# A float32 product with the values for all sixteen units of the first chunk, and a later due step for the values' halves, in a clustered attention with an MLP

## The chip, the cores and the metric

The kernel runs on one core of a Trainium2 chip. The metric is the device time of one execution in microseconds (us), as a median of runs. The engines are named as the profile names them: PE is TensorE (matmul; PEld its weight loads), DVE is VectorE, ACT is ScalarE, POOL is GpSimd, and SP issues the DMAs.

## The reference

Attention with a mask: a query sees a key only if both fall to the same of 16 centroids. Its output, of all heads side by side, goes through a two-layer MLP whose nonlinearity is a scaled square of the relu.

```
q_assign = argmax(q_n @ c_n^T); k_assign = argmax(k_n @ c_n^T)    # q_n, k_n, c_n: normalised
mask = q_assign[:, :, :, None] == k_assign[:, :, None, :]
scores = where(mask, scale * (q @ k^T), -1e9)
attn = exp(scores - max(scores)); attn = attn / (sum(attn) + 1e-9)
x = (attn @ v) of all heads, reshaped to 3072 x 512
h = x @ w_in; r = max(h, 0); g = s * r * r + b; out = g @ w_out
```

Sizes: q, k and v have 4 batches, 8 heads, 768 positions and 64 elements a head; w_in is 512 x 2048 and w_out 2048 x 512. All is float32.

## The kernel before

**Units.** The attention is cut into 192 units of 128 queries of one head, in the order batch b, chunk c (256 positions, three a batch), head pair hp, tile t, head h. Sixteen units make a chunk of the MLP's input: 256 rows of x, 512 columns, of which each group of four units (one head pair) yields 128. The main loop runs over steps i. Step i takes the scores of unit i (L476: 4 matmuls of float16 halves, with the mask folded into them as a large number), their maxima (L486, DVE) and the exponentials p (L496, ACT).

**The MLP.** With a lag of 21 steps (`LAG`) a step of the MLP runs beside a unit: 192 steps, 16 for each chunk, one 128-column slice of the hidden layer each (`mlp_in` L632, `mlp_relu` L639 to L642, `mlp_gl` L647, `mlp_out` L659). The first step of a chunk needs x of all its four head pairs, and `mlp_start` (L617 to L623), which makes scales from the maxima of x.

**Float16 in halves.** What is multiplied is mostly split into a high and a low float16 half, with a power of two as scale, and three products of halves replace one in float32. The weights are fetched in 32 pieces (SP), rebased (L215, ACT), narrowed (L219 and L220, DVE) and bounded (L227 and L229, ACT, with L232 on PE for w_in). When all are bounded, their scale is set (L254 to L259 for w_in, L263 to L269 for w_out, small instructions on DVE), and from step 17 on each is split (`wsplit`: L277 on ACT, L279 on DVE, two pairs a step for 16 steps).

**The values.** `prep_v` loads v (tiles `vn`, four head pairs of two heads), takes the maximum, and splits each pair into `vh` (L194, ACT) and `vl` (L196, DVE). For the first batch the raw `vn` are also kept as `VN`.

**Probabilities times values.** Three forms of it exist:

- Units 0 to `RAW` - 1, that is 0 to 3 here: p is turned by six PE transposes in float32 into `turned` (L520, two halves of three), each half is copied into the float32 tile `PT` (first half by DVE, second by ACT, L126 and L128 in the helper `copy`), and six float32 matmuls a unit multiply it with `VN` (L542). The sum of p comes out of the exponentials as a second output of ACT, read by an extra instruction; `finish_x` scales the group's x by an extra ACT instruction (L592).
- Units `RAW` to `TURN` - 1, 4 to 15: p is turned in the same way, but each half is copied to a float16 high half by ACT (L525), and DVE subtracts that from `turned` for the low half (L526). Eighteen float16 matmuls a unit (L547 to L549) use `vh` and `vl`; a column of ones in `vh` gives the sum.
- Units from 16 on: p is split by ACT or POOL or DVE (L126, L128, L528) and turned by a DMA; `value` (L574 to L576) follows.

`values` takes two units at a time, four steps behind (L555, L556 and L559 on DVE normalise). `finish_x` then splits x (L596 ACT, L599 POOL), turns it by a DMA (L602) and takes its maximum (L105).

**What sets the order.** A scheduler that simulates the program's time writes each engine's queue; the engines run their queues in order, and tiles come out of pools with fixed numbers of buffers. The two lines that say when the halves of the values are due are of `prep_v`: for batch 0 the pairs go in the order 1, 2, 3, 0, one a step; for later batches a pair waits for its step, `yield from until(...)`, in which a generator gives its turn back until the loop's step counter is there.

Of the kernel before, what the change touches and what calls it, by code (L numbers as in the profile page):

```python
# [26 lines left out]
def tile_cluster_attention_mlp(ctx, tc, q, k, v, cent, w_in, w_out, s_in, b_in, out):  # L27
# [5 lines left out]
    NP = H // 2  # L33
# [9 lines left out]
    LAG = 21  # L43
    BIGN = 11

    RAW = 4
    TURN = 16
    URGENT = 20

# [10 lines left out]
    def floor2(eng, dst, src):  # L60
        eng.tensor_scalar(dst, src, 2.0 ** -60, 2.0 ** 60, op0=ALU.max, op1=ALU.min)
        eng.tensor_scalar(dst.bitcast(I32), dst.bitcast(I32), EXPMASK, None, op0=ALU.bitwise_and)

    def inverse2(eng, dst, src, e):
        eng.tensor_scalar(dst.bitcast(I32), src.bitcast(I32), -1, (254 + e) << 23, op0=ALU.mult, op1=ALU.add)
# [15 lines left out]
    def load(dst, src, free=False):  # L81
        if last_transpose[0] is None or free:
            nc.sync.dma_start(dst, src)
        else:
            with tc.issue_after(last_transpose[0].ins):
                nc.sync.dma_start(dst, src)
# [4 lines left out]
    def columns(n, name):  # L91
        return sb.tile([P, n], BF16, tag=f"amb{n}", name=f"amb_{name}", bufs=3)

    def allmax(dst, src, name, bank="m"):
        n = src.shape[1]
        if bank == "turned":
            pm = turned[:, 0]
        else:
            pm = (ps_m if bank == "m" else ps_h).tile([P, 512], F32, tag=bank, name=f"am_{name}")
        for j in range(n):  # L100
            nc.tensor.matmul(pm[:, j * P : (j + 1) * P], src[:, j : j + 1].broadcast_to([P, P]), identb, start=True, stop=True)
        V.tensor_reduce(dst, pm[:, : n * P].rearrange("p (n q) -> p n q", q=P), axis=AX.X, op=ALU.max)

    def absmax(dst, src, axis=AX.X):
        V.tensor_reduce(dst, src, axis=axis, op=ALU.max, apply_absolute_value=True)  # L105
# [18 lines left out]
    def copy(eng, dst, src):  # L124
        if eng is A:
            A.activation(dst, src, AF.Copy)  # L126
        else:
            eng.tensor_copy(dst, src)  # L128
# [58 lines left out]
    def split(hi, lo, src, f, early):  # L187
        if early:
            A.activation(src, src, AF.Copy, scale=f)
            last_split[1] = A.activation(hi, src, AF.Copy)  # L190
            yield
            G.tensor_tensor(lo, src, hi, op=ALU.subtract)
        else:
            last_split[1] = A.activation(hi, src, AF.Copy, scale=f)  # L194
            yield
            last_split[0] = V.scalar_tensor_tensor(lo, src, f, hi, op0=ALU.mult, op1=ALU.subtract)  # L196
# [112 lines left out]
    def until(k):  # L309
        while step[0] < k:  # L310
            yield
# [106 lines left out]
    def prep_v(b):  # L418
        vm = sb.tile([P, 8], F32, tag="vm", name=f"vm_{b}", bufs=2)
        VM[b] = vm  # L420
        vns = []
        for hp in range(NP):
            vn = sb.tile([P, 2, T, D], F32, tag="kv", name=f"vn_{b}_{hp}", bufs=5)
            load(vn, v[b, 2 * hp : 2 * hp + 2].rearrange("h (p t) d -> p h t d", t=T), False)
            vns.append(vn)
            if b == 0:
                VN[hp] = vn
            yield
        if b:
            yield from until(START[b][3])  # L430
        for hp in range(NP):
            absmax(vm[:, hp : hp + 1], vns[hp].rearrange("p h t d -> p (h t d)"))
            if hp < NP - 1:
                yield
        vc = columns(1, f"v{b}")
        V.tensor_reduce(vc, vm[:, 0:NP], axis=AX.X, op=ALU.max)
        if b:
            yield
        allmax(vm[:, 5:6], vc, f"v{b}")
        yield  # L440
        floor2(V, vm[:, 6:7], vm[:, 5:6])
        inverse2(V, vm[:, 7:8], vm[:, 6:7], 0)
        V.tensor_scalar(vm[:, 7:8], vm[:, 7:8], 2.0 ** 13, None, op0=ALU.mult)
        V.tensor_scalar(vm[:, 6:7], vm[:, 6:7], 2.0 ** -19, None, op0=ALU.mult)
        for hp in ((1, 2, 3, 0) if b == 0 else range(NP)):
            vh = sb.tile([P, 2, T, D + 2], F16, tag="vh", name=f"vh_{b}_{hp}", bufs=5)
            vl = sb.tile([P, 2, T, D], F16, tag="vl", name=f"vl_{b}_{hp}", bufs=5)
            VS[(b, hp)] = (vh, vl)
            G.memset(vh[:, :, :, D:], 1.0)
            yield from split(vh[:, :, :, :D], vl, vns[hp], vm[:, 7:8], False)  # L450
            if b == 0 or hp < NP - 1:
                yield
                if b > 0:
                    yield from until(48 * b - 8 + 4 * hp)
# [33 lines left out]
    def exps(i):  # L488
# [5 lines left out]
        p = sb.tile([P, S], F32, tag="big", name=f"p_{i}", bufs=BIGN)  # L494
        total = {"accum_out": sm[:, 2, j : j + 1]} if i < RAW else {}
        last_exp[0] = A.activation(p.rearrange("p (a b) -> p a b", a=2), u["sc"], AF.Exp, bias=bi, scale=u["scale"], **total)  # L496
# [11 lines left out]
    def low(i):  # L508
        u = U[i]
        if i < TURN:  # L510
            n = T // 2
            flat = sb.tile([P, T * P], F32, tag="big", name=f"PT_{i}", bufs=BIGN) if i < RAW else None
            two = None if i < RAW else sb.tile([P, 2, T * P], F16, tag="big", name=f"PT_{i}", bufs=BIGN)
            if i < RAW:
                u["PT"] = flat.rearrange("p (n q) -> p n q", n=T)
            else:
                u["PT"] = two.rearrange("p e (n q) -> p (e n) q", q=P)
            for e in range(2):
                for kt in range(n):
                    nc.tensor.transpose(turned[:, e, kt * P : (kt + 1) * P], u["p"][:, (e * n + kt) * P : (e * n + kt + 1) * P], ident)  # L520
                cols = slice(e * n * P, (e + 1) * n * P)
                if i < RAW:
                    copy((V, A)[e], flat[:, cols], turned[:, e, : n * P])
# [8 lines left out]
    def values(i):  # L532
# [3 lines left out]
        for e in range(2):  # L536
            b, c, hp, t, h = units[i + e]
            PT = U.pop(i + e)["PT"]
            o = px[:, e * W : e * W + D]
            if i < RAW:  # L540
                for kt in range(T):
# [144 lines left out]
    for b in range(B):  # L686
        for c in range(NCH):
            for hq in range(2):
                s0 = ((b * NCH + c) * 2 + hq) * 8 - 10
                if s0 > 0:  # L690
                    at(s0, prep_q(b, c, hq))
        if b > 0:
            at(START[b][0], prep_k(b, 0))
            at(START[b][1], prep_v(b))
            for hp in range(1, NP):
                at(48 * b - 24 + 6 * hp + (hp == NP - 1), prep_k(b, hp))
# [13 lines left out]
    def prepare(k):  # L710
# [4 lines left out]
        with behind(last_score[0], last_exp[0], last_max[0]):  # L715
# [9 lines left out]
            if k == 4:  # L725
                some(first_v, 1)
                active.append(first_v)

    first_v = prep_v(0)
    first_k = [prep_k(0, hp) for hp in range(NP)]  # L730
    first_q = [prep_q(0, 0, hq) for hq in range(2)]
# [91 lines left out]
```

## Time and profile before

| | |
|---|---|
| runs | 946.06, 946.23, 949.96 us; median 946.23 |
| profiled execution | 952.97 us, its span 951.3 us |
| busy in the span | PE 830.0 us (87%), ACT 715.4 (75%), DVE 651.1 (68%), POOL 548.0 (58%) |
| mean granted clock of PE | 0.954 of full speed |

A row of a group gives line, engine, operation, tiles written and read, shapes and count, then busy time and the mean length in ns, then the idle time of the engine just ahead of these instructions, with what ended most of it. A row of the timeline gives start and length in us; what stands in brackets is the idle time before it and what ended that. In the chain of work that ended last, each row is a piece of the path that led to the end. The page's forty slices of the span show how the start differs from the rest:

```profile
PE   0565667886999889999999989999999899999997
DVE  7689978798786766758967766667877565654100
PEclk9975697999999999999999999999999999999999
```

Each digit is a fortieth of the span (23.8 us) in tenths, of busy time, and in the last row of the clock that PE was granted.

### The profile page before, as it was taken

Reading aid. Unit: us, or ns where it says so; the run is one execution under the profiler, and the core shown is the slowest. Engines: PE = TensorE matmul, PEld = TensorE weight load, DVE = VectorE, ACT = ScalarE, POOL = GpSimd, SP = SyncE. Lnnn points to the kernel's source line nnn. Section 1 sums busy time; section 2 is a strip of 40 time slices with the busy share of each in tenths; the row PEclk is TensorE's granted clock in tenths of the full one; section 3 lists DMA queues with packets and bytes.
Section 4 is the critical chain, followed back from the end, with each engine's and each line's share of the span. In section 5 each row is a group of like instructions: output and inputs, shape, how many; then the busy total and the mean of one; then the engine's idle time right before and its main releaser. Section 6 shows DMA issues by size and latency. Waiting matters only on the chain.

```text
span 951.3 us, 22936 instructions
## 1 busy us (share of the span) xinstructions
PE 830.0 (87%) x8697; PEld 580.1 (61%) x8697; DVE 651.1 (68%) x1684; ACT 715.4 (75%) x1405; POOL 548.0 (58%) x580
## 2 busy tenths in 40 slices
PE   0565667886999889999999989999999899999997
PEld 0353445554676657767666657667766676676764
DVE  7689978798786766758967766667877565654100
ACT  3469866777688678788878868888888788888543
POOL 3010115667577567677677747767776676666321
PEclk9975697999999999999999999999999999999999
DMA  5898513767897897876887978979968777577200
GB/s 165 215 262 283 161 38 80 174 145 150 168 168 146 172 204 123 167 162 139 178 169 164 201 156 148 171 145 197 178 140 182 145 123 159 115 140 140 46 23 23
DMA packets 437759, 144.25 MB, mean 152 GB/s; under 512 B 405392, under 2 KB 434064, under 8 KB 437648
## 3 DMA queue, kind: packets, MB, share of 16 engines
q1 hardware_dynamic: 437648, 142.78, 70.7%
q8 instruction: 68, 1.11, 0.5%
q14 instruction: 43, 0.35, 0.1%
HBM read 35.69 MB, written 6.29 MB: 44 GB/s over the span
## 4 chain that ended last, share of the span: by engine, by line
PE 45%; DVE 23%; DMA 12%; ACT 7%; issue 5%; POOL 2%; SPq 1%; POOLq 0%; DVEq 0%; ACTq 0%
PE h L632 16%; PE acc L659 16%; PE sc L476 6%; DVE ssm L486 5%; DMA qn<-in_q_dram 3%; DMA PT<-ph 2%; PE sc L574 2%; DMA kn<-in_k_dram 2%; DMA vn<-in_v_dram 2%; PE sc L576 2%; PE sc L575 2%; ACT p L496 1%; DVE wis L279 1%; DVE qa L196 1%; DMA wst<-in_moe_w_in_dram 1%
## 5 line engine op out<-in xcount | busy, mean ns | idle before, releaser
L528 POOL TENSOR_TENSOR ph<-p,ph 128x768 f16<-128x768 f32 x176 | 297.0, 1688 | 129.7 <-ACT ph L126 71.1
L632 PE MATMUL h<-x,wis 128*128 128x256 f16 x2304 | 291.9, 276 | 16.1 <-ACT r L639 9.7
L659 PE MATMUL acc<-wos,gs 128*128 128x512 f16 x1152 | 299.7, 381 | 4.1 <-POOL gs L647 2.8
L632 PEld LDWEIGHTS <-wis 128*128 128x128 f16 x2304 | 222.5, 99 | 72.3 <-issue 18.0
L496 ACT ACTIVATE p<-sc,ssm,qsm 128x768 f32<-128x768 f32 x192 | 188.5, 982 | 2.0
L647 POOL TENSOR_TENSOR gs<-r,gs 128x256 f16<-128x256 f32 x192 | 136.5, 712 | 88.1 <-ACT r L642 79.4
L486 DVE TENSOR_REDUCE ssm<-sc 128x1 f32<-128x768 f32 x192 | 181.7, 947 | 2.8 <-PE sc L476 2.6
L659 PEld LDWEIGHTS <-gs 128*128 128x128 f16 x1152 | 101.4, 98 | 79.4 <-POOL gs L647 5.6
L493 ACT ACTIVATE ssm<-ssm,lift,qsm 128x1 f32<-128x1 f32 x192 | 73.1, 381 | 91.3 <-DVE ssm L486 90.1
L126 ACT ACTIVATE ph<-p 128x768 f16<-128x768 f32 x164 | 136.7, 833 | 1.3 <-DMA PT<-ph 0.2
L639 ACT ACTIVATE r<-h,cf 128x256 f32<-128x256 f32 x192 | 89.2, 465 | 57.8 <-PE h L632 54.5
L574 PE MATMUL sc<-vh,PT 128*128 128x65 f16 x1032 | 117.4, 195 | 6.9 <-DMA PT<-ph 6.8
L576 PE MATMUL sc<-vh,PT 128*128 128x65 f16 x1032 | 117.9, 193 | 0.0
L575 PE MATMUL sc<-vl,PT 128*128 128x64 f16 x1032 | 117.5, 192 | 0.0
L476 PE MATMUL sc<-KA,QA 128*128 128x384 f16 x384 | 98.9, 340 | 19.2 <-ACT p L496 13.8
L574 PEld LDWEIGHTS <-PT 128*128 128x128 f16 x1056 | 99.1, 98 | 22.8 <-DMA PT<-ph 10.1
L575 PEld LDWEIGHTS <-PT 128*128 128x128 f16 x1056 | 98.5, 99 | 11.8 <-issue 0.5
L476 PE MATMUL sc<-KB,QB 128*128 128x384 f16 x384 | 99.2, 340 | 6.9 <-DMA QB<-qb 6.9
L576 PEld LDWEIGHTS <-PT 128*128 128x128 f16 x1056 | 98.7, 97 | 1.3
L580 DVE TENSOR_SCALAR ssm<-sc 128x1 f32<-128x1 f32 x172 | 26.1, 152 | 84.5 <-PE sc L576 83.7
L642 ACT ACTIVATE r<-r 128x256 f32<-128x256 f32 x192 | 78.8, 410 | 2.9
L641 ACT ACTIVATE gs<-r 128x256 f16<-128x256 f32 x192 | 78.9, 411 | 2.7
(176 smaller groups left out, 1145.0 us busy)
## 6 DMA issues: line engine op xcount, KB each, us to landing
wst<-in_moe_w_in_dram SPq DMA_DIRECT2D x16, 512.0 KB, 5.1
kn<-in_k_dram SPq DMA_DIRECT2D x16, 384.0 KB, 4.3
qn<-in_q_dram SPq DMA_DIRECT2D x24, 256.0 KB, 3.3
vn<-in_v_dram SPq DMA_DIRECT2D x16, 384.0 KB, 4.3
out_dram<-o SPq DMA_DIRECT2D x12, 512.0 KB, 3.6
wst<-in_moe_w_out_dram SPq DMA_DIRECT2D x8, 512.0 KB, 5.7
gs<-in_moe_w_out_dram SPq DMA_DIRECT2D x8, 512.0 KB, 4.9
PT<-ph SPq DMA_TRANSPOSE x176, 3.4
```

What stands on the lines that cost most here:

```text
L126: A.activation(dst, src, AF.Copy)
L476: last_score[0] = nc.tensor.matmul(sc[:, e, :HALF], X[:, col, :], y[:, h * S + e * HALF : h * S + (e + 1) * HALF], start=st, stop=not st)
L486: last_max[0] = V.tensor_reduce(SM[i // 4][:, 0, j : j + 1], U[i]["sc"], axis=AX.XY, op=ALU.max, negate=True)
L496: last_exp[0] = A.activation(p.rearrange("p (a b) -> p a b", a=2), u["sc"], AF.Exp, bias=bi, scale=u["scale"], **total)
L528: G.tensor_tensor(u["ph"][:, 1, :], u["p"], u["ph"][:, 0, :], op=ALU.subtract)
L574: nc.tensor.matmul(o1, PT[:, kt, :], vh[:, h, kt, : D + 1], start=(kt == 0), stop=False)
L575: nc.tensor.matmul(o, PT[:, kt, :], vl[:, h, kt, :], start=False, stop=False)
L576: nc.tensor.matmul(o1, PT[:, T + kt, :], vh[:, h, kt, : D + 1], start=False, stop=(kt == T - 1))
L632: nc.tensor.matmul(ph[:, :CW], WSP[ft][0][:, wl, kt, :], XS[(b, c, kt)][:, :, xl, :], start=(i == 0), stop=(i == len(terms) - 1))
L639: A.activation(r, ph[:, :CW], AF.Relu, scale=MS[(b, c)][0])
L647: G.tensor_tensor(g[:, 1, :], r, g[:, 0, :], op=ALU.subtract)
L659: nc.tensor.matmul(acc[:, t, :], g[:, gl, rows], WSP[ft][1][:, wl, :], start=(ft == 0 and gl + wl == 0), stop=(ft == NF - 1 and gl == 1))
```

## The change

`RAW` becomes 16, the value of `TURN`. So all sixteen units of the first chunk take the first of the three forms: their halves of `turned` are copied once instead of copied and subtracted, `PT` is float32, six float32 matmuls a unit take the place of eighteen in float16, the sums come with the exponentials, and x of all four groups is scaled in `finish_x`. The second form has no unit left. For batch 0, `prep_v` takes the head pairs in the order 0 to 3, and the halves of pair hp are due from step `RAW - 2 + 2 * hp` on, that is 14, 16, 18 and 20; the last pair of batch 0 no longer yields behind its split. The first unit that uses the halves is unit 16, of pair 0.

```diff
-    RAW = 4
+    RAW = 16
...
-        for hp in ((1, 2, 3, 0) if b == 0 else range(NP)):
+        for hp in range(NP):
+            if b == 0:
+                yield from until(RAW - 2 + 2 * hp)
             vh = sb.tile([P, 2, T, D + 2], F16, tag="vh", name=f"vh_{b}_{hp}", bufs=5)
             vl = sb.tile([P, 2, T, D], F16, tag="vl", name=f"vl_{b}_{hp}", bufs=5)
...
-            if b == 0 or hp < NP - 1:
+            if hp < NP - 1:
                 yield
```

The lines below it in the file stand two lines lower afterwards (L526 becomes L528, and so on). Where the change moves instructions in the engines' queues is shown at the places that the prediction speaks of.

## The prediction

> **What bounds the kernel now.** I first cut the run into stretches and read each engine's busy time there (columns: start and end, length, then busy time and instruction count of each engine, the granted TensorE clock, DMA share and GB/s).
>
> ```profile
> core 0: us, PE busy (x) PEld busy (x) DVE busy (x) ACT busy (x) POOL busy (x), PEclk, DMA share, GB/s
> 60.00:117.60 57.60, 35.02 (x284) 27.04 (x284) 50.78 (x132) 47.45 (x98) 6.12 (x8) 0.59 0.75 222
> 117.60:151.20 33.60, 20.08 (x203) 13.95 (x203) 27.16 (x69) 20.63 (x39) 8.79 (x8) 0.80 0.19 43
> 151.20:232.00 80.80, 68.42 (x696) 45.83 (x695) 70.71 (x152) 60.57 (x119) 50.66 (x44) 0.95 0.65 140
> 232.00:951.30 719.30, 684.80 (x7304) 478.79 (x7304) 455.32 (x1209) 557.06 (x1096) 470.54 (x476) 0.99 0.74 147
> ```
>
> From 232 us on TensorE is busy for 684.80 of 719.30 us: that part has its own length and follows the MLP's start. Before it VectorE (DVE) is the fullest engine, and TensorE is idle for 36.1 of the 91.2 us from 60.00 to 151.20. The cuts are events of the timeline:
>
> ```profile
> 113.30 0.67 DVE L220 SCALAR_TENSOR_TENSOR wo<-gs,wo 128x512 uint32<-128x512 uint32 x1
> 116.82 0.14 DVE L259 TENSOR_SCALAR glob<-glob 128x1 f32<-128x1 f32 x1
> 147.53 1.20 SPq L602 DMA_TRANSPOSE x<-xn  x1
> 151.18 0.46 ACT L639 ACTIVATE r<-h,cf 128x256 f32<-128x256 f32 x1
> ```
>
> The last weight is narrowed at 113.30 and the scale of w_in stands at 116.82, yet the MLP's first relu runs at 151.18, behind the transpose of x at 147.53: x of units 12 to 15 comes last, not the weights. The chain of work that ended last shows why, in a piece from between:
>
> ```profile
> 120.67 0.48 ACT PT L525
> 121.17 0.57 DVE PT L526
> 121.79 0.56 PE turned L520 x3
> 122.37 0.50 ACT PT L525
> 122.89 0.56 DVE PT L526
> 123.45 0.86 DVE ssm L486
> 124.31 0.16 DVE ssm L555
> 124.50 0.17 DVE ssm L556
> 124.66 0.52 DVE PT L526
> 125.23 0.55 PE turned L520 x3
> ```
>
> Each half of a unit's probabilities goes TensorE, ScalarE (ACT), VectorE and back, with nothing beside it: 121.17 to 122.89 is 1.72 us a half, 3.4 a unit, and VectorE's queue lies in that loop.
>
> **The change, part by part.** Prices are from the groups by line and shape from 36 to 160 us (count, busy us, mean ns, idle time ahead):
>
> ```profile
> L486 DVE TENSOR_REDUCE ssm<-sc 128x1 f32<-128x768 f32 x21 | 19.9, 949 | 2.8 <-PE sc L476 2.6
> L526 DVE TENSOR_TENSOR PT<-turned,PT 128x384 f16<-128x384 f32 x24 | 13.2, 550 | 2.4 <-ACT PT L525 2.3
> L525 ACT ACTIVATE PT<-turned 128x384 f16<-128x384 f32 x24 | 11.6, 483 | 7.4 <-PE turned L520 6.5 <-DVE glob L62 0.8
> L128 DVE COPY PT<-turned 128x384 f32<-128x384 f32 x4 | 2.2, 547 | 1.8 <-PE turned L520 1.8
> L126 ACT ACTIVATE PT<-turned 128x384 f32<-128x384 f32 x4 | 1.9, 476 | 0.7 <-PE turned L520 0.7
> L496 ACT ACTIVATION_READ_ACCUMULATOR p<-sc,ssm,qsm 128x1 f32 x4 | 0.8, 192 | 0.0
> L592 ACT ACTIVATE xs<-xs,vm 128x256 f32<-128x256 f32 x1 | 0.5, 493 | 0.0
> ```
>
> Neighbours on an engine overlap a little, so I charge the distance of starts:
>
> ```profile
> 126.45 0.56 DVE L526 TENSOR_TENSOR PT<-turned,PT 128x384 f16<-128x384 f32 x1
> 126.93 0.95 DVE L486 TENSOR_REDUCE ssm<-sc 128x1 f32<-128x768 f32 x1
> 127.79 0.14 DVE L65 TENSOR_SCALAR glob<-glob 128x1 int32<-128x1 int32 x1
> ```
>
> that is 0.48 for a half's turn and 0.86 for a reduce, both about 0.1 under their lengths.
>
> *VectorE.* 24 subtractions leave, 12 plain copies come, at one price each: 12 x 0.48 = 5.8 us less.
>
> *ScalarE.* 24 copies become 12 (-12 x 0.38), 12 exponentials get a sum to read (12 x 0.11), three groups of x a scaling (3 x 0.4): -4.6 + 1.3 + 1.2 = -2.1 us. It was busy for 68.1 of 91.2 us, so it does not become the bound; the scaling of the last group, 0.5 us, stands in the last x's way and is charged.
>
> *TensorE.* Of the two products, the float32 one (22 of a line in a row) and the first and last of 36 float16 ones:
>
> ```profile
> 64.24 4.84 PE L542 MATMUL px<-vn,PT 128*128 128x64 f32 x22
> 115.39 0.26 PE L547 MATMUL px<-vh,PT 128*128 128x65 f16 x1
> 117.31 0.24 PE L549 MATMUL px<-vh,PT 128*128 128x65 f16 x1
> ```
>
> 0.22 us each against (117.31 - 115.39)/35 = 0.055: 72 x 0.22 - 216 x 0.055 = 15.8 - 11.9 = +4.0 us. It lies in TensorE's 36.1 idle us, so I cost it at nothing; without that cover it is 4.0.
>
> *The values' halves* do not move, whatever their due step. VectorE's queue before (vl_0_1 is the low half of head pair 1 of batch 0, wo6 a weight, px a product with the values):
>
> ```order
> L220 SCALAR_TENSOR_TENSOR wo6_678<-wst_13_679,wo6_678 128x512
> L196 SCALAR_TENSOR_TENSOR vl_0_1_771<-vn_0_1_451,vm_0_250,vh_0_1_770 128x768
> L196 SCALAR_TENSOR_TENSOR vl_0_2_886<-vn_0_2_527,vm_0_250,vh_0_2_885 128x768
> L559 TENSOR_TENSOR xs_0_716<-px_2_818,ssm_0_389 128x128
> L233 TENSOR_REDUCE w1_129<-pw_3_619 128x1
> L196 SCALAR_TENSOR_TENSOR vl_0_3_1032<-vn_0_3_596,vm_0_250,vh_0_3_1031 128x768
> ```
>
> and now, at the same weight:
>
> ```order
> L220 SCALAR_TENSOR_TENSOR wo6_678<-wst_13_679,wo6_678 128x512
> L196 SCALAR_TENSOR_TENSOR vl_0_0_1218<-vn_0_0_251,vm_0_250,vh_0_0_1217 128x768
> L196 SCALAR_TENSOR_TENSOR vl_0_1_1332<-vn_0_1_451,vm_0_250,vh_0_1_1331 128x768
> L128 COPY PT_5_752<-turned_135 128x384
> L561 TENSOR_TENSOR xs_0_714<-px_2_808,ssm_0_389 128x128
> L196 SCALAR_TENSOR_TENSOR vl_0_2_1401<-vn_0_2_527,vm_0_250,vh_0_2_1400 128x768
> ```
>
> The scheduler puts them where their operands are ready; only their order among themselves differs. Price: nothing. The raw values are held longer, until units 12 to 15 are done; the next load into their pool came at 171.72, well after that.
>
> ```profile
> 171.72 0.50 SPq L86 DMA_DIRECT2D kn<-in_k_dram  x1
> ```
>
> *What the scheduler did move* is the units, ahead of the weights. VectorE's queue before, around the scale of w_in (L258 and L259; wis0 is the first scaled weight, sc_14 unit 14's scores):
>
> ```order
> L526 TENSOR_TENSOR PT_10_1072<-turned_135,PT_10_1072 128x384
> L258 TENSOR_SCALAR glob_131<-glob_131 128x1
> L259 TENSOR_SCALAR glob_131<-glob_131 128x1
> L555 TENSOR_SCALAR ssm_8_869<-px_8_1240 128x2
> L556 RECIPROCAL ssm_8_869<-ssm_8_869 128x2
> L279 SCALAR_TENSOR_TENSOR wis0_1536<-wi0_257,glob_131,wis0_1536 128x512
> L559 TENSOR_TENSOR xs_2_1279<-px_8_1240,ssm_8_869 128x128
> L526 TENSOR_TENSOR PT_10_1072<-turned_135,PT_10_1072 128x384
> L486 TENSOR_REDUCE ssm_12_1153<-sc_14_1308 128x1
> ```
>
> and now (amb_q0_1_1 is the maximum of the next chunk's q):
>
> ```order
> L105 TENSOR_REDUCE amb_q0_1_1_1275<-qn_0_1_1_1221 128x2
> L62 TENSOR_SCALAR glob_131<-glob_131 128x1
> L557 TENSOR_SCALAR ssm_12_1077<-ssm_12_1077 128x2
> L65 TENSOR_SCALAR glob_131<-glob_131 128x1 x2
> L558 RECIPROCAL ssm_12_1077<-ssm_12_1077 128x2
> L258 TENSOR_SCALAR glob_131<-glob_131 128x1
> L259 TENSOR_SCALAR glob_131<-glob_131 128x1
> L267 TENSOR_SCALAR glob_131<-glob_131 128x1
> L268 TENSOR_SCALAR glob_131<-glob_131 128x1
> L269 TENSOR_TENSOR glob_131<-sv_253,glob_131 128x1
> L488 TENSOR_REDUCE ssm_16_1317<-sc_17_1342 128x1
> ```
>
> When L259 comes, 17 units have been reduced instead of 14, and units 14 and 15 are still to be turned instead of 10 to 15 (two VectorE copies against twelve subtractions).
>
> *The sum.* Ahead of L259 VectorE gets 3 reduces more (+2.6), 2 turns fewer (14 instead of 16, -1.0), 2 pairs' normalisations (three small instructions, 0.36: +0.7), a maximum of x and that of q (+0.9) and w_out's small steps (+0.5): +3.7 us. Of its 57.60 - 50.78 = 6.8 idle us I take 2 back, since a half now crosses two engines instead of three; the bounds are none and all. From L259 to the first relu it loses the same three reduces, pairs, maxima and steps (4.7), 10 turns (4.8) and one weight's half that moves behind (0.7): -10.2. Of its 33.60 - 27.16 = 6.4 idle us, 2.3 stood ahead of subtractions (L526 above, behind ScalarE's copy), and 2.27 behind a load:
>
> ```profile
> 131.14 0.69 DVE L105 TENSOR_REDUCE amb_q<-qn 128x2 bf16<-128x512 f32 x1 [2.27 <-DMA qn<-in_q_dram]
> ```
>
> I take 3.3 back (the first, and half of the second). Unit 15's own loop needs two units of two halves at about 1.2 us (0.56 + 0.5 and a handoff), under 5 us of the 20 that are left, so it no longer binds. In all +3.7 - 2 - 10.2 - 3.3 + 0.5 = **-11.3 us** for the first relu, and for the end, which hangs on it. The profiled execution took 952.97 us, its span 951.3: 941.7. It lies 6.7 us over the median of the runs, 946.23; on that scale the forecast is **934.9, say 935 us**.
>
> **The rivals.** (The measurement can tell about 0.5%, 4.7 us, from no change.)
>
> 1. *Only the removed work counts*: handoffs cost as much idle time as before. 5.8 - 0.5 = 5.3 us, 940.9. For it: VectorE was 88% busy up to 117.60. Against: the loop's strict alternation above.
> 2. *All idle time goes too*: a further 1.5 + 6.4 us or so, to 19 us, 927. Against it: loads of weights still arrive one by one.
> 3. *A load takes the stall's place*: L105 on q now stands ahead of L259, and everything behind it (every weight's scaling) waits for qn, whose buffer comes free with unit 8's products. If VectorE's 2.27 us become a whole landing (3 to 5 us) plus the queue's delay, 7 to 9 us are lost: 942 to 944, no change.
> 4. *Slower: TensorE's clock.* It was 0.59 and 0.80 in the first two stretches, 0.95 in the third. If the third fell to 0.59, its 68.42 us would become 110, 29 more than the 80.8 us there, less the 11.3 gained: 964. It decides from 0.67 (68.42 x 0.95/0.67 = 97 us, 11.3 + 4.7 over 80.8). Against it: that stretch keeps its instructions, and TensorE was 85% busy there.
>
> The row for the clock's cause is an idle time in the first stretch:
>
> ```profile
> 74.25 0.61 PE L232 MATMUL pw<-wab,ones 128*128 128x128 bf16 x4 [3.79 <-DVE w L233]
> ```
>
> The Trainium skill, "TensorE: Matmul & The Clock Gate", Part 1: The HAM clock gate, says that TensorE falls to half rate after an idle window of about 3.4 us and returns after a busy one. By that rule the trace agrees: the low clock is where such gaps are, 0.99 where TensorE is full; and it would make rival 4 happen only if the change opened such gaps behind 151 us.
>
> **How the numbers follow.** Forecast (7 to 16 us gained) 0.56; rival 1 0.13; rival 2 0.08; rival 3 0.15; rival 4 0.08. Rival 1 lies at the bound of 941.5 and is split: faster 0.56 + 0.08 + 0.10 = 0.74; same 0.03 + 0.15 = 0.18, and slower 0.08. The range takes rivals 1 to 3 in, from a gain of 20 us to none, 926 to 946, and 2 us on either side, since the runs shown lie up to 3.7 us off their own median: 924 to 948. It leaves out rival 4 and little else.
>
> **What would show it.** Right: no L525 and L526 left at the first chunk, a half's loop near 1.2 us, the first relu near 140 instead of 151.18 with L259 near 118 to 119, VectorE's idle time between the two under 4 us, and from 232 us on the same length of the rest. Wrong: L259 later than 122, or L105 on q waiting over 5 us ahead of it (rival 3); a clock under 0.8 after the first relu (rival 4); or a first relu that is early and steps behind it that are longer, which would mean that the scaling of the weights on VectorE, not x, sets the first sixteen steps.

## The result, and the profile after

| | before | after |
|---|---|---|
| median of 14 runs each, us | 949.19 | 953.55 |
| ratio, 95% interval | | 1.0053 [1.0033, 1.0073] |
| profiled execution (span), us | 952.97 (951.3) | 951.90 (950.2) |

The forecast was 935 us, a gain. The change gains nothing; if it does anything, it costs half a per cent. (The three runs shown first had a median of 946.23; all 14 have 949.19.) The ratio is of the fast runs alone: it leaves out one run before of 4655.46 us and one after of 961.32.

The windows of the changed kernel, with the prediction's stretches and columns:

```profile
core 0: us, PE busy (x) PEld busy (x) DVE busy (x) ACT busy (x) POOL busy (x), PEclk, DMA share, GB/s
60.00:117.60 57.60, 44.39 (x244) 35.76 (x244) 46.74 (x117) 43.05 (x93) 5.93 (x8) 0.55 0.78 222
117.60:151.20 33.60, 26.00 (x175) 20.75 (x176) 25.16 (x71) 21.86 (x44) 8.23 (x8) 0.76 0.17 40
151.20:232.00 80.80, 64.56 (x691) 43.52 (x690) 71.14 (x153) 60.35 (x119) 53.27 (x45) 0.99 0.63 141
```

VectorE's busy time up to 151.2 us fell by 50.78 + 27.16 - 46.74 - 25.16 = 6.0 us, very near the 5.8 forecast. In the same two stretches TensorE's rose by 44.39 + 26.00 - 35.02 - 20.08 = 15.3 us, where 4.0 were forecast.

The groups by line and shape from 36 to 160 us show why. First the kernel before:

```profile
L520 PE MATMUL turned<-ident,p 128*128 128x128 f32 x96 | 22.4, 356 | 14.2 <-DVE PT L526 9.6 <-ACT p L496 2.1 <-ACT PT L126 1.7
L476 PE MATMUL sc<-KA,QA 128*128 128x384 f16 x42 | 13.5, 412 | 10.2 <-ACT p L496 10.2
L542 PE MATMUL px<-vn,PT 128*128 128x64 f32 x48 | 8.6, 339 | 0.0
```

Then the changed kernel (lines two higher):

```profile
L544 PE MATMUL px<-vn,PT 128*128 128x64 f32 x192 | 34.0, 346 | 1.7 <-DVE xs L561 1.7
L522 PE MATMUL turned<-ident,p 128*128 128x128 f32 x96 | 23.0, 364 | 11.6 <-DVE PT L128 7.1 <-ACT p L498 2.1 <-ACT PT L126 2.0
L488 DVE TENSOR_REDUCE ssm<-sc 128x1 f32<-128x768 f32 x22 | 20.8, 951 | 8.7 <-PE sc L478 8.7
L128 DVE COPY PT<-turned 128x384 f32<-128x384 f32 x16 | 8.8, 549 | 5.5 <-PE turned L522 4.1 <-ACT p L498 1.4
```

Sixteen units of six transposes are x96: one record for each. But four units of six float32 products were x48 before, and sixteen are x192 now: **each float32 product is two records**. And VectorE now waits for TensorE: its reduces wait 8.7 us for scores (2.6 before), its copies 4.1 us for `turned`. How that comes about stands in the timeline of the changed kernel (in brackets the idle time ahead of an instruction):

```profile
94.28 3.94 PE L544 MATMUL px<-vn,PT 128*128 128x64 f32 x18
98.02 0.85 PE L522 MATMUL turned<-ident,p 128*128 128x128 f32 x3
98.66 1.38 PE L544 MATMUL px<-vn,PT 128*128 128x64 f32 x6
98.87 0.66 ACT L215 ACTIVATE wi<-wst 128x512 f32<-128x512 f32 x1 [2.47 <-DMA wst<-in_moe_w_in_dram]
99.56 0.43 DVE L219 TENSOR_SCALAR wi<-wi 128x512 int32<-128x512 int32 x1 [2.25 <-ACT wi L215]
99.90 0.55 DVE L128 COPY PT<-turned 128x384 f32<-128x384 f32 x1
100.51 0.90 PE L522 MATMUL turned<-ident,p 128*128 128x128 f32 x3
...
112.22 0.68 DVE L220 SCALAR_TENSOR_TENSOR wo<-gs,wo 128x512 uint32<-128x512 uint32 x1
117.01 0.56 DVE L128 COPY PT<-turned 128x384 f32<-128x384 f32 x1 [2.21 <-PE turned L522]
126.16 0.68 DVE L105 TENSOR_REDUCE amb_q<-qn 128x2 bf16<-128x512 f32 x1
127.14 0.14 DVE L259 TENSOR_SCALAR glob<-glob 128x1 f32<-128x1 f32 x1
...
138.87 1.38 PE L544 MATMUL px<-vn,PT 128*128 128x64 f32 x6
140.04 0.85 PE L478 MATMUL sc<-KA,QA 128*128 128x384 f16 x2
140.68 0.85 PE L478 MATMUL sc<-KB,QB 128*128 128x384 f16 x2
141.57 0.96 DVE L488 TENSOR_REDUCE ssm<-sc 128x1 f32<-128x768 f32 x1 [3.12 <-PE sc L478]
146.33 1.19 SPq L604 DMA_TRANSPOSE x<-xn  x1
150.32 0.46 ACT L641 ACTIVATE r<-h,cf 128x256 f32<-128x256 f32 x1
```

A block of 18 product records holds TensorE for 3.94 us, and the three transposes of the next half stand behind it. Two things lie between that half and the other one, at 100.51: six more product records, and VectorE's copy at 99.90, which stood in its queue behind the first pass of a narrowing (L219) that waited, by way of L215, for a weight's load. At 138.87 six product records stand directly ahead of the scores, for which VectorE's reduce then waits 3.12 us. The last narrow came at 112.22, 1.1 us earlier than before; but the scale of w_in (L259) at 127.14 is 10.3 us later, and the first relu at 150.32 only 0.9 earlier.

### The profile page after: what moved, and what is told of

Read it like the earlier page. It is cut to its first block, busy times and chain, and to the rows that moved or that the text cites. A ratio compares the mean times of both kernels' runs of the same rounds, so it can differ in the third digit from the quotient of the medians.

```text
span 950.2 us, 22788 instructions
## 1 busy us (share of the span) xinstructions
PE 840.6 (88%) x8625; PEld 593.4 (62%) x8625; DVE 639.2 (67%) x1672; ACT 712.0 (75%) x1408; POOL 548.2 (58%) x580
## 5 line engine op out<-in xcount | busy, mean ns | idle before, releaser
L634 PE MATMUL h<-x,wis 128*128 128x256 f16 x2304 | 290.5, 274 | 12.5 <-ACT r L641 6.5
L495 ACT ACTIVATE ssm<-ssm,lift,qsm 128x1 f32<-128x1 f32 x192 | 73.0, 380 | 75.4 <-DVE ssm L488 74.2
L582 DVE TENSOR_SCALAR ssm<-sc 128x1 f32<-128x1 f32 x172 | 26.3, 153 | 93.9 <-PE sc L578 92.7
```

What stands on the lines that cost most here:

```text
L634: nc.tensor.matmul(ph[:, :CW], WSP[ft][0][:, wl, kt, :], XS[(b, c, kt)][:, :, xl, :], start=(i == 0), stop=(i == len(terms) - 1))
```

## The experiments

One number sorts them. The **head** is the time of the fourth chunk's first relu (the 49th step of the MLP); the **tail** is what is left of the span. The change's own instructions all lie in the head. Times in us, from each profiled execution; ratios to the kernel before, from several runs each. Two profiles of the kernel before differ by 1.8 us at the first relu, 0.8 in the head and 3.1 in the tail, so smaller differences between two single profiles tell nothing.

| kernel | ratio [95%] | L259 | first relu | head | tail |
|---|---|---|---|---|---|
| before | | 116.8 | 151.2 | 385.9 | 565.4 |
| c_before | 0.9998 [0.9973, 1.0023] | 114.0 | 149.4 | 385.1 | 562.3 |
| after | 1.0053 [1.0033, 1.0073] | 127.1 | 150.3 | 381.3 | 568.9 |
| c_after | 1.0040 [1.0013, 1.0068] | 126.1 | 149.3 | 380.6 | 570.3 |
| e1_product_only | 1.0048 [1.0024, 1.0073] | 125.8 | 148.9 | 379.9 | 566.0 |
| e2_one_copy_f16 | 0.9997 [0.9977, 1.0016] | 117.7 | 137.0 | 375.7 | 567.7 |
| c_e2 | 0.9961 [0.9937, 0.9985] | 116.7 | 136.6 | 374.6 | 568.2 |
| e4_product_third | 0.9906 [0.9876, 0.9936] | 121.0 | 140.8 | 371.9 | 565.1 |
| e3_product_twice | 1.0188 [1.0129, 1.0248] | 136.2 | 162.0 | 393.8 | 568.2 |
| e5_product_behind | 1.0001 [0.9971, 1.0030] | 122.2 | 156.0 | 387.3 | 562.4 |
| e7_split_before | 0.9837 [0.9800, 0.9874] | 126.0 | 139.5 | 366.3 | 562.0 |
| e8_split_after | 0.9766 [0.9719, 0.9813] | 127.9 | 145.6 | 365.7 | 558.2 |
| e10_acc_only | 0.9998 [0.9976, 1.0020] | 114.4 | 148.7 | 382.5 | 565.0 |
| e11_acc_only_after | 0.9955 [0.9928, 0.9981] | 125.6 | 148.8 | 382.0 | 557.7 |
| e12_tail60_before | 0.9920 [0.9894, 0.9947] | | 150.6 | 386.1 | 556.7 |
| e13_tail60_after | 0.9980 [0.9946, 1.0014] | | 151.4 | 383.0 | 563.5 |
| e12_tail140_before | 0.9959 [0.9936, 0.9983] | | 150.8 | 386.8 | 558.5 |
| e13_tail140_after | 0.9976 [0.9946, 1.0005] | | 149.7 | 381.5 | 562.0 |

### The change in its parts: c_after and e1

c_after is the changed kernel again. e1 is the changed kernel with the order and the due steps of the values' halves as before:

```diff
-        for hp in range(NP):
-            if b == 0:
-                yield from until(RAW - 2 + 2 * hp)
+        for hp in ((1, 2, 3, 0) if b == 0 else range(NP)):
...
-            if hp < NP - 1:
+            if b == 0 or hp < NP - 1:
                 yield
```

> The changed kernel once more, for a second profile of it. Theory A (the float32 products cost TensorE 144 recorded matmuls of 0.22 us against 216 of 0.055, 31.7 against 11.9 us, and stand in its queue ahead of the turns) and every rival: the first relu at 149 to 152 us, the scale of w_in (L259) at 125 to 129, 1.002 to 1.008 of the time before.

> RAW is 16, but the values' halves are made in the old order and from the old step. Theory A: the same as the change, first relu at 149 to 152 us, 1.002 to 1.008. Rival (the later due step or the longer life of the raw values costs the gain): first relu near 140 us, 0.985 to 0.993.

1.0040 and 1.0048 on the same chip, heads 380.6 and 379.9: the due step of the halves costs and brings nothing that these runs can tell. What happens comes with `RAW`, that is with the product, the plain copies, the sums and the scaling.

### VectorE's relief without the product: e2 and c_e2

The kernel before, where units 4 to 15 copy a half of `turned` once, into the float16 high half, alternately by DVE and ACT. The low half of p is left out, and the third set of products reads the high half again, so TensorE's work is that of before.

```diff
                 else:
-                    A.activation(two[:, 0, cols], turned[:, e, : n * P], AF.Copy)
-                    V.tensor_tensor(two[:, 1, cols], turned[:, e, : n * P], two[:, 0, cols], op=ALU.subtract)
+                    copy((V, A)[e], two[:, 0, cols], turned[:, e, : n * P])
...
-                nc.tensor.matmul(o1, PT[:, T + kt, :], vh[:, h, kt, : D + 1], start=False, stop=(kt == T - 1))
+                nc.tensor.matmul(o1, PT[:, kt, :], vh[:, h, kt, : D + 1], start=False, stop=(kt == T - 1))
```

> From the kernel before: for units 4 to 15 each half is copied once to float16 (VectorE the first, ScalarE the second, as in the change) and the low half of p is left out; the eighteen float16 matmuls stay, the third set reading the high half again. So VectorE and ScalarE are relieved as in the change, and TensorE's work stays as before. Theory A: the forecast gain appears, first relu at 138 to 143 us, 0.986 to 0.992. Rival B (the turned halves' loop never set the first relu; weights or the load of q do): first relu at 148 to 152, 0.997 to 1.003. Rival C (the scheduler's order, units ahead of weights, costs it): L259 at 125 or later all the same.

> The kernel e2_one_copy_f16 once more. If the part of its early first relu that is missing at the end is lost by the program: first relu at 136 to 138 us, about 4 to 5 us of the 14 lost by the 33rd relu, 0.998 to 1.002 again. If by chance of the run: the ratio comes out near 0.990.

The timeline of e2 (a line lower than before behind L526):

```profile
117.72 0.14 DVE L259 TENSOR_SCALAR glob<-glob 128x1 f32<-128x1 f32 x1
137.00 0.45 ACT L638 ACTIVATE r<-h,cf 128x256 f32<-128x256 f32 x1
```

Without a longer product L259 comes near 118 and the first relu 12.4 us ahead of c_before's 149.42 (12.8 in c_e2), about what the forecast gave the change. As in the changed kernel, VectorE reduces 17 units ahead of L259 here; so that order of units and weights is not what makes L259 late there.

Yet the ratio, expected at 0.986 to 0.992, is 0.9997 in one set of runs and 0.9961 in the other: an early first relu is not an early end. (One program in two sets of runs differs by 0.4% here.) Of the 14.2 us that the first relu is ahead of the profile before, 10.2 are left in the head, and the tail gives 2.3 back. What the head lost went in the second chunk's steps, from its first relu (the 17th) to the third chunk's: they take 80.8 us in e2 and 80.4 in c_e2, and 75.4 in the kernel before. Which wait makes them longer is not shown.

### More and less of the product: e4 and e3

e4 leaves out four of the six float32 products of each unit; e3 does all six twice.

```diff
-                for kt in range(T):
-                    nc.tensor.matmul(o, PT[:, kt, :], VN[hp][:, h, kt, :], start=(kt == 0), stop=(kt == T - 1))
+                for kt in range(0, T, 3):
+                    nc.tensor.matmul(o, PT[:, kt, :], VN[hp][:, h, kt, :], start=(kt == 0), stop=(kt == 3))
```

```diff
-                for kt in range(T):
-                    nc.tensor.matmul(o, PT[:, kt, :], VN[hp][:, h, kt, :], start=(kt == 0), stop=(kt == T - 1))
+                for _ in range(2):
+                    for kt in range(T):
+                        nc.tensor.matmul(o, PT[:, kt, :], VN[hp][:, h, kt, :], start=(kt == 0), stop=(kt == T - 1))
```

> The change with two of six float32 matmuls of each unit (the other four are left out of the product). Theory A: TensorE loses 128 of 192 recorded matmuls, 28 us at 0.22 us; first relu at 138 to 143 us, 0.986 to 0.992. Rivals B and C: as the change, first relu at 148 to 152, 1.000 to 1.008.

> The change with every float32 product of the first sixteen units computed twice (same result). Theory A: 192 recorded matmuls more, 21 us at full clock and 42 us at half; most of it shows, first relu at 165 to 190 us, 1.015 to 1.045. Rival B (the product lies in TensorE's idle time): first relu at 150 to 155, 1.000 to 1.010.

The first relu in the timeline of e4:

```profile
140.84 0.45 ACT L641 ACTIVATE r<-h,cf 128x256 f32<-128x256 f32 x1
```

and in that of e3:

```profile
162.04 0.46 ACT L642 ACTIVATE r<-h,cf 128x256 f32<-128x256 f32 x1
```

Against 150.32 that is -9.5 us for 128 records fewer and +11.7 for 192 more: about a third of their 28 and 42 us at 0.22 us each. (For e3 at least 165 was expected.) So TensorE's products, which were to be hidden, stand on the path of the first relu, though not with all their time. The heads differ by -9.4 and +12.5, but e3's does not carry its late first relu on: at the second chunk's first relu e3 is 3.6 us behind the changed kernel, and 9.6 more come in that chunk's steps, 80.9 us against 71.3, as in e2.

### Another place in the queue: e5

The products are ordered behind the newest unit's transposes, so that no block stands between the two halves of a turn:

```diff
-                    nc.tensor.transpose(turned[:, e, kt * P : (kt + 1) * P], u["p"][:, (e * n + kt) * P : (e * n + kt + 1) * P], ident)
+                    last_T[0] = nc.tensor.transpose(turned[:, e, kt * P : (kt + 1) * P], u["p"][:, (e * n + kt) * P : (e * n + kt + 1) * P], ident)
...
-                values(i - 5)
+                with behind(last_T[0]):
+                    values(i - 5)
```

> The change with the products of a pair ordered behind the turns of the newest unit, no longer between the two halves of a turn. Theory A with the place in the queue as the cause: first relu at 141 to 146 us, 0.990 to 0.997. Theory A with the amount of work as the cause: first relu at 147 to 152, 1.000 to 1.008.

L259 came 5 us earlier than in the changed kernel and the first relu 5.7 later, at 156.0, where one theory had 141 to 146 and the other 147 to 152. VectorE waits less for the scores, as its reduces' group shows (36 to 160 us; e5's lines are one more than the changed kernel's):

```profile
L489 DVE TENSOR_REDUCE ssm<-sc 128x1 f32<-128x768 f32 x22 | 20.9, 952 | 4.5 <-PE sc L479 4.5
```

But the products come later and in whole blocks. A block can still hold the next unit's turn, as at 93.16, and the last pair's block stands shortly ahead of the last transpose of x, in the timeline:

```profile
93.16 5.22 PE L545 MATMUL px<-vn,PT 128*128 128x64 f32 x24
98.38 0.85 PE L523 MATMUL turned<-ident,p 128*128 128x128 f32 x3
...
140.39 5.38 PE L545 MATMUL px<-vn,PT 128*128 128x64 f32 x24 [3.34 <-DVE xs L562]
...
151.57 1.21 SPq L605 DMA_TRANSPOSE x<-xn  x1
```

4.5 us of waiting instead of 8.7, and the transpose of x at 151.57 instead of 146.33. The place of a block chooses who waits for it; its length stays. The head of 387.3 has another source: at the second chunk's first relu, 240.5, e5 is 2.3 us ahead of the changed kernel, and that chunk's steps then take 80.9 us against 71.3. Why is open, as in e2 and e3.

### Two tiles for the two halves: e7 and e8, e10 and e11

`turned` is one tile of two banks; a half's transposes wait for the other half's copy (9.6 us behind the subtractions before, 7.1 behind the copies after, in the groups above). e7 (the kernel before) and e8 (the changed kernel) give each half a tile of its own; the MLP's accumulator `acc`, which shares the space, becomes two tiles too:

```diff
-    turned = ps_a.tile([P, CT, DM], F32, tag="acc", name="turned")
+    turned = [ps_a.tile([P, DM], F32, tag=f"acc{e}", name=f"turned{e}") for e in range(2)]
...
-                    nc.tensor.transpose(turned[:, e, kt * P : (kt + 1) * P], u["p"][:, (e * n + kt) * P : (e * n + kt + 1) * P], ident)
+                    nc.tensor.transpose(turned[e][:, kt * P : (kt + 1) * P], u["p"][:, (e * n + kt) * P : (e * n + kt + 1) * P], ident)
...
-            MS[(b, c)][2] = ps_a.tile([P, CT, DM], F32, tag="acc", name=f"acc_{n}")
+            MS[(b, c)][2] = [ps_a.tile([P, DM], F32, tag=f"acc{e}", name=f"acc{e}_{n}") for e in range(CT)]
```

> The kernel before with the tile in which p is turned split into two tiles of one bank each (and the MLP's accumulator too), so that the two halves of a turn need not wait for each other. If the loop of turn, copy and subtraction sets the first relu: 140 to 146 us instead of 151, 0.988 to 0.996. If the engines' work sets it: first relu at 149 to 152, 0.998 to 1.002.

> The changed kernel with the same two tiles. Theory A (TensorE's work sets the pace): first relu at 147 to 152 us, 0.998 to 1.007. If the wait of one half for the other's copy sets it: first relu at 138 to 144, 0.986 to 0.994.

e10 and e11 are the same two kernels with both halves in `turned[0]`, so that only the accumulator has two tiles.

> The kernel before with the MLP's accumulator in two tiles of a bank, but both halves of a turn in the first of these tiles, so that the turns keep one lane. If the two lanes of the turn made e7_split_before faster: first relu at 149 to 153 us, 0.992 to 1.002. If the accumulator's two tiles did: as e7, 0.981 to 0.987, with the gain behind 151 us.

> The changed kernel in the same form, accumulator in two tiles, turns in one lane. If the lanes matter: first relu at 149 to 153 us, 0.994 to 1.005, over 1.5% above e8_split_after. If the accumulator's tiles do: 0.974 to 0.980, as e8.

The groups from 36 to 160 us, in e7:

```profile
L520 PE MATMUL turned<-ident,p 128*128 128x128 f32 x96 | 20.6, 347 | 5.8 <-DVE PT L526 3.4 <-ACT p L496 2.1 <-DVE glob L62 0.3
```

In e8:

```profile
L522 PE MATMUL turned<-ident,p 128*128 128x128 f32 x96 | 19.8, 348 | 2.7 <-ACT p L498 2.1 <-DVE PT L128 0.6
```

And in e10:

```profile
L520 PE MATMUL turned<-ident,p 128*128 128x128 f32 x96 | 22.3, 354 | 13.0 <-DVE PT L526 8.6 <-ACT p L496 2.1 <-ACT PT L126 1.9
```

With two tiles the transposes' idle time falls from 14.2 to 5.8 us (e7) and from 11.6 to 2.7 (e8), and the heads from 385.9 to 366.3 and from 381.3 to 365.7. With the accumulator alone split it is 13.0, and the head 382.5. In e11 the head is 382.0; its ratio of 0.9955 comes from a shorter tail. So it is the two lanes of the turn that gain, 1.6% in e7 against e10 and 1.9% in e8 against e11 (by the ratios of the table), more than was expected of either and more than the 1.2% (11.3 of 952.97) that the forecast gave the change; e8 is the fastest kernel of all, 926.04 us.

With the lanes apart, e8's first relu is still 6.1 us behind e7's, but the second chunk's first relu comes at 233.0 and 232.9, and the two forms of the product give the same head (365.7, 366.3); what is left between their ratios lies in their tails. L259 is as late in e7 and e8, 126.0 and 127.9, as in the changed kernel; so a late scale of w_in does not by itself keep the first relu at 150.

### The last half per cent: c_before, e12 and e13

The changed kernel's head is 4.6 us shorter than before, and its total is not. c_before is the kernel before again.

> The kernel before, as a run of its own, for a second profile. If the program sets where time goes: first relu 150 to 152 us, 143 us from there to the first step of the third chunk's MLP within 2 us, the rest from there within 3 us of 565, ratio 0.998 to 1.002. If it varies from run to run: the rest differs by over 4 us from the first profile.

From the second chunk's first relu to the fourth's c_before takes 143.2 us, where the first profile has 143.0, and the rest is 562.3 against 565.4: the program sets these times to within some 3 us.

In the windows of the kernel before, the second chunk's steps and the tail are these:

```profile
242.90:318.30 75.40, 72.69 (x790) 49.63 (x786) 57.03 (x144) 58.12 (x113) 53.15 (x56) 1.00 0.87 162
385.90:951.30 565.40, 542.43 (x5763) 380.51 (x5761) 344.80 (x922) 441.58 (x872) 364.87 (x371) 0.99 0.71 142
```

and in the changed kernel:

```profile
242.80:314.10 71.30, 70.30 (x763) 49.00 (x762) 54.56 (x138) 58.00 (x112) 53.83 (x55) 0.99 0.87 170
381.30:950.20 568.90, 542.58 (x5756) 380.32 (x5754) 337.60 (x920) 440.10 (x871) 363.71 (x371) 0.99 0.71 141
```

The head's 4.6 us come in the steps from 242.8 us on, 71.30 us where they were 75.40. In the tail TensorE's busy time is the same (542.58, 542.43); its idle time is 26.3 us, and was 23.0. In c_after and c_before the tails differ by 8.0 us. e1, which has the same product, has a tail of 566.0, near that of the kernel before. No instruction of the tail is changed, but the scheduler has written its queues in another order. e12 and e13 change only that order: the priority of the products with the values from step 72 on, in the kernel before and in the changed one, to 60 and to 140. The queues are the same up to that part.

```diff
-            with tc.high_priority(offset=100):
+            with tc.high_priority(offset=100 if i < 72 else 60):
                 value(i - 4, i)
```

> The kernel before, with the priority of the products with the values of units 68 on (steps 72 on) lowered from 100 to 60; no instruction is added or removed, and the queues are the same up to about unit 70. The tail is the time from the fourth chunk's first relu to the end (562.3 and 565.4 us in two profiles of the kernel before, 568.9 and 570.3 after the change). Theory A, the tail's length is a matter of the order that the scheduler happens to write: the tail moves by several us (out of 562 to 566) though nothing else changes, in either direction. Theory B, the tail's loss is a fixed cost of the change: this kernel's tail stays at 562 to 566 us and the ratio within 0.998 to 1.002. The head (first relu of the fourth chunk) stays at 385 to 386 us by both.

> The same lowered priority (60 from step 72 on) in the changed kernel. Theory A: the tail moves off 569 to 570 us by several us, and the difference from the kernel before with the same priority is not the +3.5 to +8 us seen so far. Theory B: tail 568 to 571 us, ratio 1.003 to 1.007. The head stays at 380 to 382 us by both.

> The kernel before with that priority raised from 100 to 140 from step 72 on (the queues are the same up to about unit 110). Theory A: a tail out of 562 to 566 us. Theory B: 562 to 566 us, ratio within 0.998 to 1.002. Head 385 to 386 us.

> The changed kernel with that priority at 140 from step 72 on. Theory A: the tail moves off 569 to 570 us, and if it comes to 562 to 566 us the total is about 4 us under the kernel before (ratio near 0.996). Theory B: tail 568 to 571 us, ratio 1.003 to 1.007. Head 380 to 382 us.

The tail of the kernel before with 60, in the windows:

```profile
386.07:942.80 556.73, 539.56 (x5763) 379.01 (x5761) 342.54 (x922) 444.98 (x872) 363.37 (x371) 1.00 0.73 144
```

and of the changed kernel with 60:

```profile
382.96:946.50 563.54, 540.13 (x5756) 378.87 (x5754) 342.68 (x920) 453.05 (x871) 363.81 (x371) 1.00 0.71 142
```

The same instructions in another order take 556.7 or 558.5 us where they took 562.3 to 565.4, and 563.5 or 562.0 where they took 568.9 to 570.3. Of the 8.7 us that 60 takes off the tail of the kernel before, 5.8 are idle time of TensorE (17.2 us, was 23.0). So the tail's length is a matter of its order, by 4 to 9 us in these profiles, the size of the result. By the runs of the kernel before only the ratio of 0.9920 stands clear: 0.9959 is as near to 1 as c_e2's 0.9961, and that program gave 0.9997 too. The changed kernel's tail is longer by 3.5, 8.0, 6.8 and 3.5 us in the four pairs with one tile of `turned`, and shorter by 3.8 and 7.3 us in e8 against e7 and in e11 against e10. With the same priority the changed kernel takes 1.006 (60) and 1.002 (140) of the kernel before, by the ratios of the table. It is no fixed price of the product, then, since the sign turns with the tiles; but the theory of the order had also expected the distance between the two kernels to leave 3.5 to 8 us, and it did not. Whether the change pushes the scheduler towards worse orders with one tile, or four pairs fell the same way by accident, stays open, and so does which wait of the order costs it.

## Why the prediction was wrong, step by step

- *VectorE: "12 x 0.48 = 5.8 us less".* Right: 6.0. Its split at L259 was off by a turn: in the kernel before 17 of 28 turns stand ahead of L259, not 16, so 0.5 us belongs on the other side of it. The sum stays.
- *ScalarE: -2.1 us.* Right in sign; it is 3.2 (47.45 + 20.63 - 43.05 - 21.86).
- *TensorE: "72 x 0.22 - 216 x 0.055 = 15.8 - 11.9 = +4.0 us".* **This term was mis-sized.** 0.22 us is the time of a record, and a product is two. So 144 records more are 31.7 us, and the term is +19.8 at the low clock, against the 15.3 measured in the two windows, where a part of the records ran at the full clock (13 in 1.56 us from 118.66 on, 0.12 each). The row that tells it, x48 for four units of six products, was to be had in the view that the other prices came from. The Trainium skill, "FP8 and Floating Point Precision", TensorE Precision Notes, says that true float32 takes four passes. An estimate from it, four times the measured 0.055, is 0.22 us a product, the price that I charged. The trace shows twice that time, and decides; how many passes a product makes, no row tells.
- *"It lies in TensorE's 36.1 idle us, so I cost it at nothing."* **This cover failed.** That idle time was in large part TensorE's wait inside loops through ScalarE and VectorE (14.2 us ahead of the transposes and 10.2 ahead of the scores, from 36 to 160 us); work put there is served in the queue's order and delays the next turn. e2, e4, after and e3 put the first relu at 137.0, 140.8, 150.3 and 162.0. From e2 to the changed kernel the first relu loses 13.3 us, two thirds of the 19.8. (They differ in the sums and in the scaling of x as well, for which the forecast charged 0.5.)
- *"The values' halves do not move. Price: nothing."* The price was right, by e1.
- *L259 at 118 to 119, a half's loop near 1.2 us.* Both wrong in the changed kernel, 127.14 and (98.02 to 100.51, with a weight's load in it) 2.49 us there; L259 is at 117.7 in e2. "L259 later than 122" was the sign named for a wrong forecast; a sign, and not the cause, as e7 shows.
- *First relu: -11.3 us.* -0.9 in the changed kernel, -0.2 between c_after and c_before; -14.2 in e2 against the first profile before and -12.4 against c_before. VectorE's part was sized well, and TensorE's term took it.
- *"And for the end, which hangs on it."* **This step failed too.** In e2 14.2 us at the first relu are 10.2 in the head and 7.9 in the span of single profiles, and by the runs 0 to 0.4% of the time, at most 3.7 us. Even without the longer product the forecast for the end would have been too good. The second chunk's steps take a part of it back, and why stays open. And "from 232 us on the same length of the rest" fails: the order of the tail alone is worth 4 to 9 us.
- *Rival 3, the load of q.* No: L105 ran at 126.16 without a wait. *Rival 4, the clock.* No: 0.99 from 151.2 to 232 us, the stretch that the rival was about. (Rival 2's "1.5 + 6.4" are 4.8 + 3.1 of the idle time left; its sum is right.) What happened was no rival of mine: the price of the product itself, on a path on which I took TensorE to have time.

## What to carry to other kernels

Count the records of an operation against its number in the source before a record's length becomes its price. Idle time of an in-order engine that lies inside a loop between engines is no cover: a block put there lengthens the loop; look first at what makes the loop wait for itself, here one tile for two halves. And where a scheduler writes the queues, change only the order of the untouched part once or twice before believing a difference below one per cent.

## What the runs showed of the hardware

**A float32 product of 128x128 by 64 columns costs eight times a float16 one of 65 at the low clock.** Two records of 0.22 us stand against one of 0.055; both rows lie where 0.50 was granted. At the full clock a block in e3 gives 0.114 us a record (last lines below). In the changed kernel the weight loads of the same block take as long as the products, 4.07 us for 18 (timeline):

```profile
93.96 4.07 PEld L544 LDWEIGHTS px<-vn,PT 128*128 128x128 f32 x18 [0.17 <-issue]
```

so the load of p, not the 64 columns, may be what paces them; no run separates the two.

**The low clock held while TensorE was busy.** Windows of the changed kernel, in other stretches:

```profile
80.80:93.00 12.20, 9.83 (x47) 8.50 (x48) 9.86 (x28) 8.55 (x18) 0.00 (x0) 0.50 0.90 276
93.00:100.20 7.20, 7.20 (x36) 6.69 (x34) 4.89 (x12) 3.61 (x9) 0.00 (x0) 0.50 0.93 298
100.20:114.90 14.70, 11.46 (x65) 7.70 (x63) 12.82 (x31) 13.56 (x33) 2.84 (x4) 0.50 0.43 123
114.90:118.60 3.70, 3.60 (x33) 3.22 (x33) 1.09 (x5) 2.33 (x7) 0.00 (x0) 1.00 0.57 142
```

From 93.00 on TensorE had 7.20 us without a gap in the records and was still granted 0.50, up to 114.90. The prediction took the Trainium skill's rule ("TensorE: Matmul & The Clock Gate", Part 1: The HAM clock gate: full rate after a busy window of about 3.4 us) to agree with the trace; in this stretch, mostly float32 products, it does not. In e3 a block of such products alone ran at the full clock (timeline and windows):

```profile
145.54 5.47 PE L545 MATMUL px<-vn,PT 128*128 128x64 f32 x48
146.00:151.00 5.00, 5.00 (x51) 5.00 (x51) 4.03 (x5) 2.60 (x5) 2.65 (x2) 1.00 0.00 0
```

So they run at either clock. Whether they count less as activity than others, and what ended the low clock at 114.90, is not shown.
